# Odd third row-maximum tile of an attention loop, taken as two half-width tiles in opposite row halves

## The chip, the cores and the metric

The kernel runs on one core of a Trainium2 chip. The metric is device time in microseconds (us) of one execution. Its engines run side by side and meet at semaphores: TensorE (PE, whose weight loads the profile lists apart as PEld), VectorE (DVE), ScalarE (ACT), GpSimd (POOL) and SyncE (SP), which issues most DMAs. Matmuls write to PSUM, which the kernel divides into eight tiles of 128 partitions by 512 fp32 numbers. They are called banks below.

## The reference

```python
x = A_x                                            # 1 x 2048 x 640
g = sigmoid((x * gate_w).sum(-1, keepdims=True))
q, k, v = heads(x @ wqkv)                          # 32 heads of 20 columns
a = softmax(q @ k.T * 20 ** -0.5) @ v @ wo         # per head, 2048 queries x 2048 keys
u = gelu(einsum("bsd,sf->bdf", layernorm(x), w1) + b1)   # over the token axis, 1728 wide
b = einsum("bdf,fs->bds", u, w2) + b2
return g * a + (1 - g) * transpose(b)
```

Everything is fp32. The kernel writes a number as the sum of a high and a low part of a shorter type (fp32r) where the product must stay exact.

## The kernel before

The kernel has four stages: the projections q, k and v; the token MLP; the attention loop; and the output projection. The 32 heads are treated as 16 pairs (`NP`). The two heads of a pair (`j` = 0 and 1) lie in rows 0 to 63 and 64 to 127 of every stacked operand, so a matmul of head 0 uses the upper half of TensorE's rows and one of head 1 the lower half. Such matmuls can run beside each other.

**Scores twice.** The softmax subtracts each query's maximum. The scores are therefore computed once with queries on the partitions, only to find the maximum ("s" tiles, line 178: 128 queries by 512 keys, reduced along the keys by VectorE on line 180). They are computed a second time with keys on the partitions ("st" tiles, line 700), with the negative maximum as two extra rows of the operand, and go to ScalarE for the exponential (line 703). The results `p` are multiplied with v (line 637, "pv"). A pair has 128 s tiles in two halves of queries (64 each), four key chunks (`kc`) for each of eight query tiles (`t`), and two heads. The maxima go to `mx`, are folded by `s_max` (lines 139 to 146), transposed by `s_store`, stored to DRAM and loaded by `load_m` as rows of the operand of the st matmuls.

**The stream of s tiles.** `s_tiles` (line 167) is a generator of closures. Each issues one matmul and one reduction, and `s_next` (line 155) runs the next one, then counts down the delayed steps in `s_close`. The first 736 of the 2048 tiles (`S_AHEAD`) are issued in the MLP, two at a time between the MLP's matmuls. The remaining 1312 (`LEFT`) are issued in the attention loop.

**The attention loop.** It has 16 pairs by 32 iterations, each with four st tiles (two heads `j` by two query chunks `c`) and four exponentials. `take` s tiles are put between the st tiles: 344 iterations take three, 140 take two, and the last 28 none. `turn` (line 708) keeps the row halves of successive matmuls alternating when an odd number was issued. After the four st tiles `pv_flush` issues eight pv matmuls with the exponentials of the iteration before. These use all 128 rows. Every 16th iteration a pv accumulation ends and `pv_evac` (line 618) copies it out on VectorE.

**Order and banks.** TensorE, VectorE, ScalarE, GpSimd and SyncE run in the order in which the code is written, so a waiting instruction holds all that is behind it on its engine. Of the eight banks `st_tile` has four, `s_tile` three, and pv one. A pool hands its banks round in turn: the fourth s tile counted from a given one takes its bank again, and its matmul waits for the reduction of the former tile. In an iteration with `take` under three, the third st tile takes a bank of the s pool, so that this pool is used three times in each iteration that takes two or three.

The lines that matter are these:

```python
def s_tile(shape, name):
    return psum.tile(shape, F32, tag="s", bufs=3, name=name)
...
for n in range(4):
    st_op((n + turn) % 2, n // 2, s_tile if n == 2 and take < 3 else st_tile)
    if n < take:
        s_next()
```

Of the kernel before, what the change touches and what calls it, by code (L numbers as in the profile page):

```python
# [7 lines left out]
F32 = mybir.dt.float32  # L8
F32R = mybir.dt.float32r
AF = mybir.ActivationFunctionType  # L10
OP = mybir.AluOpType
AX = mybir.AxisListType

P = 128
S, D, H, DH, F = 2048, 640, 32, 20, 1728
# [13 lines left out]
def gated_mix(ctx, tc, xT, x, wqk, wv0, wv1, wo, w1, w1t, b1, w2, b2, out):  # L29
    nc = tc.nc  # L30
# [5 lines left out]
    def hi_lo(hi, lo, src, hi_eng=None, lo_eng=None):  # L36
        if hi_eng is nc.scalar:
            nc.scalar.activation(hi, src, AF.Copy)  # L38
        else:
            (hi_eng or nc.vector).tensor_copy(hi, src)  # L40
        (lo_eng or nc.vector).tensor_sub(lo, src, hi.bitcast(F32))  # L41
# [22 lines left out]
    cp = ctx.enter_context(tc.tile_pool(name="cp", bufs=1))  # L64
# [3 lines left out]
    def st_tile(shape, name):  # L68
        return psum.tile(shape, F32, tag="st", bufs=4, name=name)

    def s_tile(shape, name):
        return psum.tile(shape, F32, tag="s", bufs=3, name=name)
# [44 lines left out]
    def base_stack(p, full, eng=nc.sync):  # L117
        ks = k8([P, S], F32R, f"ks{p}_{full}")
        qs = [q4([P, S // 2], F32R, f"qs{p}_{full}_{i}") for i in range(2)]
        load_stack(p, ks, qs, full, eng)  # L120
        return ks, qs

    def load_m(p, qs, half, put=nc.sync.dma_start):
        src = m_d[p, half].rearrange("(g i j t) r -> i j t g r", i=2, j=2, t=8)
        for j in range(2):
            for i in range(2):
                r = 64 * j + 3 * DH + i
                dst = qs[half].bitcast(F32)[r: r + 1, :].rearrange("o (t g r) -> o t g r", g=4, r=32)
                put(dst, src[i: i + 1, j])

    s_src, st_src, v_tiles = {}, {}, {}

    def load_v(p):
        v_tiles[p] = base.tile([P, NT, NPAIR], F32, tag="v", bufs=2, name=f"v{p}")
        c0 = NPAIR * (p % 8)
        nc.sync.dma_start(v_tiles[p], v_d[p // 8, :, :, c0: c0 + NPAIR].rearrange("t p c -> p t c"))

    s_close = []

    def s_max(p, half, mx):  # L140
        mm = cp.tile([P, 16], F32, tag="mm", bufs=2, name=f"mm{p}_{half}")
        mc = cp.tile([P, 32], F32R, tag="mc", bufs=2, name=f"mc{p}_{half}")
        nc.vector.tensor_reduce(mm, mx.rearrange("p k j t -> p (j t) k"), axis=AX.X, op=OP.max)
        nc.gpsimd.tensor_scalar_mul(mm, mm, -1.0)
        hi_lo(mc[:, :16], mc[:, 16:], mm, hi_eng=nc.gpsimd, lo_eng=nc.gpsimd)
        s_close.append([8, lambda: s_store(p, half, mc)])

    def s_store(p, half, mc):
        mt = cp.tile([P, 32], F32, tag="mt", bufs=2, name=f"mt{p}_{half}")
        nc.vector.transpose(mt, mc.bitcast(F32))  # L150
        s_close.append([M_LAG[0], lambda: m_queue[0].dma_start(m_d[p, half], mt)])

    M_LAG = [8]

    def s_next():
        next(stream)()
        for e in list(s_close):
            e[0] -= 1
            if e[0] <= 0:
                s_close.remove(e)  # L160
                e[1]()

    def s_finish():
        next(stream, None)
        while s_close:
            s_close.pop(0)[1]()

    def s_tiles(p):
        for half in range(2):
            mx = cp.tile([P, 4, 2, 8], F32, tag="mx", bufs=2, name=f"mx{p}_{half}")  # L170
            for t in range(8):
                for kc in range(4):
                    for j in (1, 0):
                        def f(j=j, kc=kc, t=t):
                            ks, qs = s_src[p]
                            ps = s_tile([P, 512], f"s{p}_{half}_{t}_{j}_{kc}")
                            r = slice(64 * j, 64 * j + 3 * DH)
                            nc.tensor.matmul(ps, qs[half][r, t * P:(t + 1) * P], ks[r, kc * 512:(kc + 1) * 512],  # L178
                                             start=True, stop=True)
                            nc.vector.tensor_reduce(mx[:, kc, j, t: t + 1], ps, axis=AX.X, op=OP.max)  # L180
                        yield f
            s_close.append([2, lambda p=p, half=half, mx=mx: s_max(p, half, mx)])

    def s_stream(on_start):
        for p in range(NP):
            on_start(p)
            yield from s_tiles(p)

    hooks = [None]
    m_queue = [nc.gpsimd]  # L190
    stream = s_stream(lambda p: hooks[0](p))

    p1s = ExitStack()
# [99 lines left out]
    for half in range(2):  # L293
        wvh, wvl = wvs[half]
        width = HALF + 2 if half == 0 else HALF
        for t in range(NT):
            n = NT * half + t
# [9 lines left out]
            ps = st_tile([P, width], f"v{half}_{t}")  # L307
# [256 lines left out]
    while done < S_AHEAD:  # L564
        s_next()
        done += 1
# [7 lines left out]
    def s_stack(p):  # L574
        ks = lp.tile([P, S], F32R, tag="sk", bufs=2, name=f"sk{p}")
        qs = [lp.tile([P, S // 2], F32R, tag="sq", bufs=4, name=f"sq{p}_{i}") for i in range(2)]
        load_stack(p, ks, qs, False)
        return ks, qs
# [52 lines left out]
    def pv_flush():  # L631
        while pend:
            p, qh, kt, pv, pts = pend.pop(0)
            for j in range(2):
                for c in range(2):
                    r = 32 * (2 * j + c)
                    nc.tensor.matmul(pv[r: r + 32, :], v_tiles[p][:, kt, 10 * j: 10 * j + 32], pts[j, c],  # L637
                                     start=(kt == 0), stop=(kt == NT - 1))
            if kt == NT - 1:
                pv_evac(p, qh, pv)  # L640
# [4 lines left out]
    def load_wo(c):  # L645
        raw = ap.tile([P, D], F32, tag="wor", bufs=1, name=f"wor{c}")
        nc.gpsimd.dma_start(raw, wo[c * P:(c + 1) * P, :])
        hi_lo(woh[c], wol[c], raw, hi_eng=nc.gpsimd, lo_eng=nc.gpsimd)
# [15 lines left out]
    def o_early(q, hi_eng=nc.scalar, lo_eng=nc.vector):  # L664
        o_hl[q] = o_part(q, slice(0, (NC - 1) * P), NC - 1, 256, "e", 2, hi_eng, lo_eng)
# [1 line left out]
    def o_late(q):  # L667
        return o_part(q, slice((NC - 1) * P, D), 1, 512, "l", 4, nc.scalar, nc.vector)[0]

    turn = given = 0  # L670
    LEFT = NP * 128 - S_AHEAD
    for p in range(NP):
        ks, qs = st_src[p]
        if 8 <= p < 8 + NC:
            load_wo(p - 8)
        for it in range(32):
            qh, kt = divmod(it, NT)
            if p + 1 < NP:
                if it == 6:
                    st_src[p + 1] = base_stack(p + 1, True)  # L680
                if it == 12:
                    load_v(p + 1)
                if it == 27:
                    load_m(p + 1, st_src[p + 1][1], 0)
            if it == 11 and p:
                load_m(p, qs, 1)
            if it == 14 and due_stack:
                n = due_stack.pop()
                if n < NP:
                    s_src[n] = s_stack(n)  # L690
            if p == NP - 1 and it in (20, 26):
                o_early(it // 26, nc.gpsimd, nc.gpsimd)
            if kt == 0:
                pv = psum.tile([P, 512], F32, tag="pv", bufs=1, name=f"pv{p}_{qh}")
            pts = {}

            def st_op(j, c, tile):
                r = slice(64 * j, 64 * j + 3 * DH + 2)
                ps = tile([P, 512], f"st{p}_{it}_{j}{c}")
                nc.tensor.matmul(ps, ks[r, kt * P:(kt + 1) * P], qs[qh][r, c * 512:(c + 1) * 512],  # L700
                                 start=True, stop=True)
                pt = lp.tile([P, 512], F32, tag="pt", bufs=12, name=f"p{p}_{it}_{j}{c}")
                nc.scalar.activation(pt, ps, AF.Exp, scale=SCALE)  # L703
                pts[j, c] = pt

            due = min((p * 32 + it + 1) * LEFT // (NP * 32 - 28) + 1, LEFT)
            take = min(due - given, 3)
            for n in range(4):
                st_op((n + turn) % 2, n // 2, s_tile if n == 2 and take < 3 else st_tile)
                if n < take:  # L710
                    s_next()
            given += take
            if take and given == LEFT:
                s_finish()
            turn = (turn + take) % 2
            pv_flush()
            if p * 32 + it in later:
                later.pop(p * 32 + it)()
            pend.append((p, qh, kt, pv, pts))
# [19 lines left out]
    for t in range(NT):  # L739
# [5 lines left out]
        ps = [st_tile([P, HALF], f"a{t}_{i}") for i in range(2)]  # L745
        a_mms(t, ps, o_hl[t // 2], slice((t % 2) * P, (t % 2 + 1) * P), range(NC - 1))
    for t in range(NT):
        ps = [st_tile([P, HALF], f"b{t}_{i}") for i in range(2)]
# [49 lines left out]
```

## Time and profile before

| | us |
|---|---|
| median of 3 runs (1844.1 to 1847.46) | 1844.79 |
| span of the profiled execution | 1844.8 |
| s tiles start (in the MLP) | 227 |
| attention loop, first to last exponential | 700 to 1762 |
| last reduction of an s tile | 1706 |
| PE busy, PEld busy | 1829.7, 1135.2 |
| VectorE busy, ScalarE busy, GpSimd busy | 1428.9, 1361.6, 637.1 |

The profiled execution is as long as the median run. TensorE shows as busy nearly throughout, but the end of a matmul is modelled and two matmuls in opposite row halves overlap, so this share says little of how full it is. The starts of the weight loads, one ahead of each matmul, show better how the matmuls follow each other. In the views, a line gives an engine, the line of the code, the operation, the tile written and those read, its shape, and how often it ran; times are in us, means of one instruction in ns. "Idle before" is the time that the engine stood still ahead of the instruction, with what ended it.

### The profile page before, as it was taken

Reading aid. Unit: us, or ns where it says so; the run is one execution under the profiler, and the core shown is the slowest. Engines: PE = TensorE matmul, PEld = TensorE weight load, DVE = VectorE, ACT = ScalarE, POOL = GpSimd, SP = SyncE. Lnnn points to the kernel's source line nnn. Section 1 sums busy time; section 2 is a strip of 40 time slices with the busy share of each in tenths; the row PEclk is TensorE's granted clock in tenths of the full one; section 3 lists DMA queues with packets and bytes.
Section 4 is the critical chain, followed back from the end, with each engine's and each line's share of the span. In section 5 each row is a group of like instructions: output and inputs, shape, how many; then the busy total and the mean of one; then the engine's idle time right before and its main releaser. Section 6 shows DMA issues by size and latency. Waiting matters only on the chain. (4 is left out here: it accounts for less than half of the span.)

```text
span 1844.8 us, 39129 instructions
## 1 busy us (share of the span) xinstructions
PE 1829.7 (99%) x14978; PEld 1135.2 (62%) x14978; DVE 1428.9 (77%) x2341; ACT 1361.6 (74%) x2688; POOL 637.1 (35%) x900
## 2 busy tenths in 40 slices
PE   9999999999999999999999999999999999999998
PEld 7998799999999994333333333333333333333378
DVE  4202299999999998888888888888888888888137
ACT  4243244465444448999999999999999999999930
POOL 1013478888887770112112111121321211212210
PEclk9999999999999999999999999999999999999999
DMA  8456766566645645504032324213540423301463
GB/s 289 143 169 212 222 173 173 158 194 193 168 139 166 189 136 121 118 15 103 20 85 61 73 42 93 57 50 78 107 103 24 109 47 77 71 14 23 131 219 132
DMA packets 152831, 216.61 MB, mean 117 GB/s; under 512 B 65698, under 2 KB 92082, under 8 KB 148738
## 3 DMA queue, kind: packets, MB, share of 16 engines
q1 hardware_dynamic: 129172, 178.68, 35.4%
q0 software_dynamic: 14688, 20.78, 5.2%
q10 hardware_dynamic: 8784, 14.65, 2.4%
q8 instruction: 118, 1.93, 0.4%
q14 instruction: 69, 0.57, 0.1%
HBM read 165.43 MB, written 48.25 MB: 116 GB/s over the span
## 5 line engine op out<-in xcount | busy, mean ns | idle before, releaser
L180 DVE TENSOR_REDUCE mx<-s 128x1 f32<-128x512 f32 x2048 | 1293.7, 684 | 159.9 <-PE s L178 119.7
L703 ACT ACTIVATE p<-st 128x512 f32<-128x512 f32 x2048 | 1042.1, 615 | 20.9 <-PE s L178 2.2
L700 PEld LDWEIGHTS st<-qs_True,ks_True 62*128 62x128 f32 x2048 | 307.3, 185 | 485.1 <-ACT p L703 312.9
L700 PE MATMUL st<-qs_True,ks_True 62*128 62x512 f32 x2048 | 579.6, 425 | 0.2 <-ACT ty L477 0.2
L637 PE MATMUL pv<-p,v 128*32 128x512 f32 x4096 | 555.5, 605 | 0.2
L178 PE MATMUL s<-sk,sq 60*128 60x512 f32 x1280 | 423.1, 434 | 0.0
L41 POOL TENSOR_TENSOR wl<-wr,wh 128x512 fp32r<-128x512 f32 x228 | 273.6, 1216 | 59.8 <-ACT wh L38 30.9
L624 POOL DMA_DIRECT2D o_d<-oev x128 | 67.0, 524 | 494.3 <-DVE oev L618 491.6
L178 PE MATMUL s<-ks_False,qs_False 60*128 60x512 f32 x768 | 225.1, 397 | 0.4 <-DVE mx L180 0.3
L46 PE MATMUL y<-gh,wh 64*128 64x320 f32 x896 | 216.8, 308 | 0.0
L46 PE MATMUL y<-gl,wh 64*128 64x320 f32 x832 | 210.3, 306 | 0.0
L46 PE MATMUL y<-gh,wl 64*128 64x320 f32 x832 | 209.4, 305 | 0.0
L38 ACT ACTIVATE wh<-wr 128x512 fp32r<-128x512 f32 (+2 forms) x246 | 135.9, 594 | 90.2 <-PE s L178 29.0
L178 PEld LDWEIGHTS s<-sk,sq 60*128 60x128 f32 x1280 | 197.7, 185 | 1.2
L637 PEld LDWEIGHTS pv<-p,v 128*32 128x32 f32 x4096 | 84.9, 108 | 171.4 <-issue 156.4
L46 PE MATMUL u<-hl,wh 64*128 64x320 f32 x864 | 167.1, 306 | 0.0
L46 PE MATMUL u<-hh,wh 64*128 64x320 f32 x864 | 167.1, 306 | 0.0
L46 PE MATMUL u<-hh,wl 64*128 64x320 f32 x800 | 156.9, 306 | 0.4 <-POOL wl L41 0.4
L46 PEld LDWEIGHTS y<-gh,wh 64*128 64x128 f32 x896 | 155.3, 184 | 0.4
L46 PEld LDWEIGHTS y<-gh,wl 64*128 64x128 f32 x832 | 147.0, 184 | 0.3
L46 PEld LDWEIGHTS y<-gl,wh 64*128 64x128 f32 x832 | 146.9, 184 | 0.0
L178 PEld LDWEIGHTS s<-ks_False,qs_False 60*128 60x128 f32 x768 | 124.4, 184 | 1.1 <-DVE mx L180 1.1
(124 smaller groups left out, 1817.6 us busy)
## 6 DMA issues: line engine op xcount, KB each, us to landing
wr<-in_w_dram SPq DMA_DIRECT2D x196, 256.0 KB
ks_True<-k_d SPq DMA_DIRECT2D x96, 160.0 KB
qs_True<-q_d SPq DMA_DIRECT2D x192, 80.0 KB
sk<-k_d SPq DMA_DIRECT2D x60, 160.0 KB
sq<-q_d SPq DMA_DIRECT2D x120, 80.0 KB
v_d<-vt SPq DMA_DIRECT2D x32, 168.0 KB
v<-v_d SPq DMA_DIRECT2D x16, 336.0 KB
xr<-in_xT_dram SPq DMA_DIRECT2D x20, 256.0 KB
```

Source lines behind the costliest of these rows:

```text
L38: nc.scalar.activation(hi, src, AF.Copy)
L41: (lo_eng or nc.vector).tensor_sub(lo, src, hi.bitcast(F32))
L46: nc.tensor.matmul(ps[k], a[r], b[r], start=start, stop=stop)
L178: nc.tensor.matmul(ps, qs[half][r, t * P:(t + 1) * P], ks[r, kc * 512:(kc + 1) * 512], start=True, stop=True)
L180: nc.vector.tensor_reduce(mx[:, kc, j, t: t + 1], ps, axis=AX.X, op=OP.max)
L624: nc.gpsimd.dma_start(o_d[DH * h: DH * h + DH, cols], ev[r: r + DH, :])
L637: nc.tensor.matmul(pv[r: r + 32, :], v_tiles[p][:, kt, 10 * j: 10 * j + 32], pts[j, c], start=(kt == 0), stop=(kt == NT - 1))
L700: nc.tensor.matmul(ps, ks[r, kt * P:(kt + 1) * P], qs[qh][r, c * 512:(c + 1) * 512], start=True, stop=True)
L703: nc.scalar.activation(pt, ps, AF.Exp, scale=SCALE)
```

## The change

An iteration that takes three s tiles now takes one full pair (both heads of one key chunk) and one half pair: 256 keys of head 0 ahead of the first st tile and the same 256 keys of head 1 behind the last one. The order in such an iteration is half (head 0), st 1, st 0, s 1, s 0, st 1, st 0, half (head 1), pv. An iteration that takes two has st 1, st 0, s 1, s 0, st 1, st 0, pv. The four st tiles always use the four banks of `st_tile`; `turn` is gone. Every tile of the s pool, a half one too, takes one of its three banks.

Only the chunks `kc` 2 and 3 are ever halved. `mx` has six columns of maxima instead of four, and a full tile of these chunks is reduced to two maxima in one instruction. Units with `kc` under 2 that `s_half` meets first are set aside in `s_skipped` and issued as the next full ones. The MLP uses the same `s_next`, so it issues the same tiles in the same order, with two-result reductions for half of them.

```diff
-    def s_next():
-        next(stream)()
+    def s_tick():
         for e in list(s_close):
             e[0] -= 1
             ...
+    def s_next():
+        if not s_one:
+            s_one.extend(s_full(s_skipped.pop(0) if s_skipped else next(stream)))
+        s_one.pop(0)()
+        s_tick()
...
+    def s_full(u):
+        def f(j):
+            ps = s_tile([P, 512], f"s{u.p}_{u.half}_{u.t}_{j}_{u.kc}")
+            u.mm(ps, j, 0, 512)
+            if u.kc < 2:
+                nc.vector.tensor_reduce(u.mx[:, u.kc, j, u.t: u.t + 1], ps, axis=AX.X, op=OP.max)
+            else:
+                nc.vector.tensor_reduce(u.mx[:, 2 * u.kc - 2: 2 * u.kc, j, u.t],
+                                        ps.rearrange("p (a b) -> p a b", a=2), axis=AX.X, op=OP.max)
+            u.ended(2)
+        return [lambda j=j: f(j) for j in (1, 0)]
+
+    def s_half():
+        while not s_rest:
+            u = next(stream)
+            if u.kc < 2:
+                s_skipped.append(u)
+            else:
+                s_rest.extend([(u, 0), (u, 1)])
+        u, h = s_rest.pop(0)
+
+        def f(j):
+            ps = s_tile([P, 256], f"s{u.p}_{u.half}_{u.t}_{j}_{u.kc}_{h}")
+            u.mm(ps, j, 256 * h, 256)
+            nc.vector.tensor_reduce(u.mx[:, 2 * u.kc - 2 + h, j, u.t: u.t + 1], ps, axis=AX.X, op=OP.max)
+            u.ended(1)
+
+        f(0)
+
+        def close():
+            f(1)
+            s_tick()
+
+        return close
...
+                mx = cp.tile([P, 6, 2, 8], F32, tag="mx", bufs=2, name=f"mx{p}_{half}")
...
-            for n in range(4):
-                st_op((n + turn) % 2, n // 2, s_tile if n == 2 and take < 3 else st_tile)
-                if n < take:
+            close = s_half() if take % 2 else None
+            for c in range(2):
+                for j in (1, 0):
+                    st_op(c, j)
+                if c == 0 and take > 1:
+                    s_next()
                     s_next()
+            if close:
+                close()
             given += take
             if take and given == LEFT:
                 s_finish()
-            turn = (turn + take) % 2
             pv_flush()
```

More of the change, by code (lines that the diff above doesn't have):

```diff
@@ L161, in s_next @@
                 e[1]()
+    def s_next():
[3 more added lines that the diff above has]
+        s_tick()
     def s_finish():
-        next(stream, None)
+        assert not s_one and not s_rest and not s_skipped
         while s_close:
             s_close.pop(0)[1]()
[L168 to L182, printed above, removed]
@@ new lines, in gated_mix, with __init__, mm, ended @@
+    s_one, s_rest, s_skipped = [], [], []
+    class Unit:
+        def __init__(self, p, half, t, kc, mx, left):
+            self.p, self.half, self.t, self.kc, self.mx, self.left = p, half, t, kc, mx, left
+        def mm(self, ps, j, lo, n):
+            ks, qs = s_src[self.p]
+            r = slice(64 * j, 64 * j + 3 * DH)
+            k0 = self.kc * 512 + lo
+            nc.tensor.matmul(ps, qs[self.half][r, self.t * P:(self.t + 1) * P], ks[r, k0: k0 + n], start=True,
+                             stop=True)
+        def ended(self, n):
+            self.left[0] -= n
+            if self.left[0] == 0:
+                s_close.append([2, lambda: s_max(self.p, self.half, self.mx)])
@@ L186, in s_stream @@
             on_start(p)
-            yield from s_tiles(p)
+            for half in range(2):
+                mx = cp.tile([P, 6, 2, 8], F32, tag="mx", bufs=2, name=f"mx{p}_{half}")
+                left = [128]
+                for t in range(8):
+                    for kc in range(4):
+                        yield Unit(p, half, t, kc, mx, left)
     hooks = [None]
@@ L668, in o_late @@
         return o_part(q, slice((NC - 1) * P, D), 1, 512, "l", 4, nc.scalar, nc.vector)[0]
-    turn = given = 0
+    given = 0
     LEFT = NP * 128 - S_AHEAD
@@ L695, in gated_mix, with st_op @@
             pts = {}
-            def st_op(j, c, tile):
+            def st_op(c, j):
                 r = slice(64 * j, 64 * j + 3 * DH + 2)
-                ps = tile([P, 512], f"st{p}_{it}_{j}{c}")
+                ps = st_tile([P, 512], f"st{p}_{it}_{j}{c}")
                 nc.tensor.matmul(ps, ks[r, kt * P:(kt + 1) * P], qs[qh][r, c * 512:(c + 1) * 512],
```

## Prediction

> **What bounds the kernel now.** I read the page's first part, then a table of stretches, then the groups and waits of 900 to 1700 us, and last the weight loads of single iterations.
>
> ```profile
> PE 1829.7 (99%) x14978; PEld 1135.2 (62%) x14978; DVE 1428.9 (77%) x2341; ACT 1361.6 (74%) x2688; POOL 637.1 (35%) x900
> ```
>
> ```profile
> core 0: us, PE busy (x) PEld busy (x) DVE busy (x) ACT busy (x) POOL busy (x), PEclk, DMA share, GB/s
> 900.00:1700.00 800.00, 799.94 (x5663) 309.70 (x5663) 678.40 (x1107) 784.56 (x1540) 150.84 (x302) 1.00 0.30 65
> 1706.50:1745.00 38.50, 38.38 (x244) 11.59 (x240) 3.82 (x6) 38.50 (x80) 12.11 (x16) 1.00 0.36 115
> ```
>
> The page's shares average over four stages; the change acts in the attention loop, so its stretch is read alone. TensorE is busy without a gap there at a granted clock of 1.00, and ScalarE for 98%. An iteration has four exponentials: 1540 are 385 iterations, 2.078 us each. Without s tiles (last stretch, about 20 iterations) four exponentials take some 1.93 us, so ScalarE is no bound until an iteration falls to about 1.93.
>
> ```profile
> L703 ACT ACTIVATE p<-st 128x512 f32<-128x512 f32 x1540 | 785.4, 604 | 15.4 <-PE s L178 0.9
> L180 DVE TENSOR_REDUCE mx<-s 128x1 f32<-128x512 f32 x1044 | 660.4, 683 | 120.6 <-PE s L178 91.9 <-PE st L700 26.4
> L618 DVE COPY oev<-pv 128x512 f32<-128x512 f32 x24 | 16.4, 682 | 1.0 <-PE pv L637 1.0
> ```
>
> ```profile
> PEld st L700 <- ACT p L703: 248.5, 370, 0.8
> PEld pv L637 <- issue: 116.5, 367, 0.4
> ...
> PEld st L700 <- DVE mx L180: 4.3, 17, 0.4
> ```
>
> VectorE waits for TensorE (120.6 us); TensorE's loads wait for VectorE only 17 times. The 248.5 us put down to ScalarE need a second look: they are the pause of 0.84 us behind the pv matmuls, and that pause is equally long where it is put down to "issue". It is the pv work itself. The loads of single iterations show this (start, length, engine, line):
>
> ```profile
> 1203.84 0.18 PEld L700 LDWEIGHTS st<-qs_True,ks_True 62*128 62x128 f32 x1 [0.84 <-ACT p L703]
> ...
> 1204.47 0.19 PEld L700 LDWEIGHTS st<-qs_True,ks_True 62*128 62x128 f32 x2 [0.34 <-DVE mx L180]
> 1204.91 0.16 PEld L637 LDWEIGHTS pv<-p,v 128*32 128x32 f32 x8 [0.25 <-issue]
> 1205.90 0.18 PEld L700 LDWEIGHTS st<-qs_True,ks_True 62*128 62x128 f32 x1 [0.84 <-issue]
> 1205.90 0.29 PEld L178 LDWEIGHTS s<-sk,sq 60*128 60x128 f32 x2
> 1206.01 0.41 PEld L700 LDWEIGHTS st<-qs_True,ks_True 62*128 62x128 f32 x2
> 1206.25 0.19 PEld L178 LDWEIGHTS s<-sk,sq 60*128 60x128 f32 x1
> 1206.48 0.18 PEld L700 LDWEIGHTS st<-qs_True,ks_True 62*128 62x128 f32 x1
> 1207.02 0.16 PEld L637 LDWEIGHTS pv<-p,v 128*32 128x32 f32 x8 [0.35 <-issue]
> 1208.02 0.18 PEld L700 LDWEIGHTS st<-qs_True,ks_True 62*128 62x128 f32 x1 [0.84 <-ACT p L703]
> ...
> 1210.15 0.18 PEld L700 LDWEIGHTS st<-qs_True,ks_True 62*128 62x128 f32 x1 [0.84 <-ACT p L703]
> ...
> 1211.05 0.16 PEld L637 LDWEIGHTS pv<-p,v 128*32 128x32 f32 x8 [0.34 <-issue]
> 1212.05 0.18 PEld L700 LDWEIGHTS st<-qs_True,ks_True 62*128 62x128 f32 x1 [0.84 <-issue]
> ...
> 1213.22 0.16 PEld L637 LDWEIGHTS pv<-p,v 128*32 128x32 f32 x8 [0.24 <-issue]
> 1214.22 0.18 PEld L700 LDWEIGHTS st<-qs_True,ks_True 62*128 62x128 f32 x1 [0.84 <-ACT p L703]
> ```
>
> An iteration is a score part, up to the pv load, and a pv part of 1.00 us (1207.02 to 1208.02, 1211.05 to 1212.05). The iteration from 1205.90 takes three s tiles: its seven matmuls go through the row halves as 0.23 us steps (loads at 1206.01, 1206.25, 1206.48), the seventh alone in its half. Its score part is 1.12 us, the whole 2.12; the next one, behind a two-tile iteration, takes 2.17 (1212.05 to 1214.22). I call these odd. The even one from 1210.15 has three pairs: 0.90 and 1.90. The mean of the odd follows from the stretch: 1044 reductions in 385 iterations are 2.71 each, so 71% are odd, and (2.078 − 0.29 × 1.90) / 0.71 = 2.15 us. **The bound is TensorE's score part**, with the lone seventh matmul in it.
>
> **The change part by part.**
>
> *Half a step less on TensorE.* With two half tiles each row half holds 3.5 matmuls, not 4 and 3. What 256 columns cost is read from matmuls of 320 and 512 in the MLP (300 to 690 us):
>
> ```profile
> L46 PE MATMUL y<-gh,wh 64*128 64x320 f32 x865 | 209.1, 307 | 0.0
> L178 PE MATMUL s<-ks_False,qs_False 60*128 60x512 f32 x610 | 183.0, 393 | 0.0
> ```
>
> 86 ns for 192 columns are 115 ns for 256. If nothing waited, an odd iteration would fall from 2.12 to 2.01 us.
>
> *A new wait.* The s pool has three banks and an odd iteration now uses four tiles of it: half 0, s 1, s 0, half 1. So half 1 always takes the bank that half 0 of the same iteration filled, and its matmul waits until VectorE has reduced that; in the built program its wait is for just that reduction. Before, three tiles used three banks, and each bank's former tile was an iteration old. I follow the wait from the first load, with these rows of VectorE:
>
> ```profile
> 1206.47 0.69 DVE L180 TENSOR_REDUCE mx<-s 128x1 f32<-128x512 f32 x1 [0.78 <-PE s L178]
> ```
>
> ```profile
> 1203.14 1.27 DVE L180 TENSOR_REDUCE mx<-s 128x1 f32<-128x512 f32 x2
> ```
>
> ```profile
> L315 DVE COPY gs<-v 128x2 f32<-128x2 f32 x16 | 2.5, 159 | 28.9 <-ACT vt L312 28.9
> ```
>
> 1. Start of the reduction of half 0: the s tile loaded at 1205.90 reached an idle VectorE at 1206.47, 0.57 later. With 256 columns less that is 0.455.
> 2. Its length is not in the trace. Copies out of PSUM take 682 ns for 512 elements and 159 for 2, thus 1.03 ns an element; 0.69 less 256 of these is 0.43, ended at 0.885. The outer ends are 0.25 (the fold of 64 numbers, quoted below, less than half its data) and 0.69 (no saving).
> 3. Release: the reduction that ended at 1203.14 + 1.27 = 1204.41 let the load of 1204.47 go, 0.06 later by these rounded rows. So half 1 loads at about 0.94. Unhindered it would load near 0.57, where the matmul ahead of it in its half begins.
> 4. From a held load to the pv load behind it: 1204.47 to 1204.91, 0.44, less 0.115: 0.325. The score part is then 1.26, and with the pv part 1.00 the iteration is **2.25 us** (2.24 to 2.26 by the rounding) against 2.15.
>
> Behind half 1 in TensorE's order stand the eight pv matmuls and all of the next iteration, so the wait is paid in full. VectorE doesn't carry a backlog that lengthens it: reductions follow each other at 0.60 (1.27 less 0.68, nearly), thus half ones at about 0.34, and s 1 and s 0 (ready from 0.8) and half 1 are done near 2.36, 0.11 into the next iteration, ahead of 0.455. So 344 × (2.25 − 2.15) = +34 us.
>
> The Trainium skill ("VectorE: DVE Perf Modes", the section on the TRN2 errata) gives VectorE 120 cycles plus one per element from PSUM at 0.96 GHz and advises tiles of 512 or more, as each small one pays the fixed part; that speaks against halves. By its figure a half takes 392 ns (an estimate), and the sum would be some 12 us lower. For 512 it gives 658 ns where the rows have 683, so I keep 0.43.
>
> *VectorE's copy ahead of half 0.* Every 16th iteration copies the pv result at the start of the next:
>
> ```profile
> 1201.95 0.68 DVE L618 COPY oev<-pv 128x512 f32<-128x512 f32 x1
> 1202.55 1.27 DVE L180 TENSOR_REDUCE mx<-s 128x1 f32<-128x512 f32 x2
> ```
>
> That iteration began at 1201.71, so reducing began at 0.84. Before, no matmul waited for it. Now half 0 starts there in place of 0.455, and half 1 is held 0.38 longer. 21 of the 31 such iterations are odd by the code's own rule of `take`: +8 us.
>
> *Even iterations.* The third st tile no longer takes a bank of the s pool. The waits of 4.3 us in 800 go; half of a 0.34 idle time is the normal cadence. I take −3 us over the loop. In exchange the four st banks wait for ScalarE: the first starts about 0.56 into an even iteration, the fourth ends 3 × 0.48 + 0.60 later, 0.70 into the next odd one, and the st tile that needs the bank would load at 0.46. That can delay its matmul to 0.85, but half 1 behind it is held to 0.94 in any case; if that cover were gone, 140 × 0.04 (the 2.17 beside 2.12) = 6 us would show.
>
> *Nothing from the rest.* The 172 halved units come from `kc` 2 and 3; each odd iteration still advances the stream by three tiles, and `s_tick` runs as often, so folds, transposes, m_d stores on GpSimd's queue and `load_m` on SP's move by an iteration or two; a single wait of 0.8 us for a load of m_d stands in the 800 us. The 344 added reductions fill VectorE's idle 120.6 us partly; that they cost no more is reckoned above. In the MLP, reductions with two results are new:
>
> ```profile
> L180 DVE TENSOR_REDUCE mx<-s 128x1 f32<-128x512 f32 x611 | 385.0, 685 | 4.3 <-PE s L178 0.5
> L143 DVE TENSOR_REDUCE mm<-mx 128x16 f32<-128x64 f32 x10 | 2.6, 256 | 0.0
> ```
>
> VectorE is 99% busy there (385 of 390 us, one in 0.638 against 0.61 back to back). 16 results of 64 numbers take 256 ns, so one result more costs a few ns: nothing. At the other end a second result costs another 159 ns, half the reductions slow the mean to 0.69, and 736 × 0.05 = 37 us come on top.
>
> **Sum** against the profiled execution (1844.8, equal to the median of the runs): 1844.8 + 34 + 8 − 3 = **1884 us**.
>
> **Rivals.**
>
> *Slower, as forecast, by 20 to 60 us: 0.82.* For it: the bank rule and five measured steps.
>
> *The wait is covered: faster.* If half 1's load were let go by 0.57 to 0.70, odd iterations would be 2.01 us, above ScalarE's 1.93, and the time 1844.8 − 344 × 0.14 − 3 = 1794 us. The deciding point is a load at 0.83: there the iteration is 0.83 + 0.325 + 1.00 = 2.15, as long as before. Against it: VectorE can start on half 0 only at 0.455, which leaves 0.37 for a reduction with its release, and my estimate is 0.49. With the outer end 0.25 the load is at 0.765, the iteration 2.09, and the total about 1829. Chance of such times 0.08.
>
> *The wait nearly evens out:* 1841 to 1849, 0.03.
>
> *Two results are dear in the MLP:* +37, thus 1921 us; against it the fold's row. 0.04. Still longer waits (VectorE carrying a backlog, a half reduction near 0.69, up to 344 × 0.26 = 90 us more): 0.03.
>
> *The change does something else:* it can't be void, since 344 more reductions and other bank uses are in the program; its cost stands in the rivals above.
>
> **How the numbers follow.** The likeliest case gives 1884. A half reduction between 0.39 and 0.46 moves it from 1870 to 1894; 0.02 us of error in each of the other three steps adds 7 us either way, and the copies may cost 0 to 12. The range 1864 to 1904 holds the main case but for its edges, about 0.8 of the chance. A measurement can tell about 0.2% (3.7 us). Faster by more than that 0.08, within 0.03, slower 0.89.
>
> **What would show it.** In the changed profile the weight loads of s (half 1) wait for the reduction, about 344 times and 0.3 us each, where 17 waits stood before; the score part of an odd iteration is about 1.26, its pv part still 1.00, an even one 1.89. Reductions of 256 take near 0.43; TensorE's loop is some 40 us longer; VectorE idles at the start of each odd iteration. The MLP ends at the same time. A half 1 that loads without a gap, or a pv part that shrinks, would prove me wrong.

## The result and the profile after

The changed kernel takes 1871.59 us (median of 4 runs, 1870.35 to 1872.37); the kernel before took 1844.44 in the same comparison. The ratio is 1.0142, 95% interval 1.0124 to 1.0159: slower by 27 us. The forecast was 1884 us, a loss of 39.

The page's first part and the stretch from 900 to 1700 us of the changed kernel (columns as in the prediction's table of stretches):

```profile
PE 1854.3 (99%) x15322; PEld 1202.2 (64%) x15322; DVE 1459.1 (78%) x2685; ACT 1361.5 (73%) x2688; POOL 636.8 (34%) x900
```

```profile
900.00:1700.00 800.00, 798.04 (x5783) 350.58 (x5782) 684.59 (x1347) 763.28 (x1501) 150.75 (x302) 1.00 0.30 65
```

There are 344 matmuls and reductions more, as the code says. TensorE is still shown as busy throughout, which does not say how full it is. ScalarE tells the loss: 1501 exponentials in 800 us where there were 1540, so an iteration takes 2.132 us on average, not 2.078. The waits of TensorE's weight loads in that stretch say for what:

```profile
PEld s L183 <- DVE mx L196: 137.8, 166, 0.8
PEld st L747 <- ACT p L750: 114.2, 210, 0.8
PEld s L183 <- DVE mx L198: 71.4, 86, 0.8
PEld s L183 <- DVE mx L215: 40.0, 161, 0.6
```

Line 215 is the new reduction of a half tile. The rows of up to 0.8 us are the pause behind pv once more, now put down to other engines. The row of line 215 counts 161 holds and 40 us. That is less than all: in the odd iterations right behind an even one (139 of 342 in the loop) the st load just ahead comes late too, waiting 0.21 us on average for ScalarE, so the held load follows it without idle time and is not counted. The time from the end of the opening half's reduction to the closing half's load shows that all are held: its median over the odd iterations is 54 ns, and nine tenths of them lie at 53 or 54. One odd iteration and the even one behind it, in weight loads and then in VectorE's instructions:

```profile
1223.22 0.18 PEld L183 LDWEIGHTS s<-sk,sq 60*128 60x128 f32 x1 [0.84 <-DVE mx L198]
1223.22 0.29 PEld L747 LDWEIGHTS st<-qs_True,ks_True 62*128 62x128 f32 x2
1223.33 0.31 PEld L183 LDWEIGHTS s<-sk,sq 60*128 60x128 f32 x2
1223.56 0.35 PEld L747 LDWEIGHTS st<-qs_True,ks_True 62*128 62x128 f32 x2
1224.12 0.18 PEld L183 LDWEIGHTS s<-sk,sq 60*128 60x128 f32 x1 [0.21 <-DVE mx L215]
1224.43 0.16 PEld L684 LDWEIGHTS pv<-p,v 128*32 128x32 f32 x8
1225.42 0.19 PEld L747 LDWEIGHTS st<-qs_True,ks_True 62*128 62x128 f32 x2 [0.84 <-ACT p L750]
...
1226.32 0.16 PEld L684 LDWEIGHTS pv<-p,v 128*32 128x32 f32 x8 [0.26 <-issue]
1227.31 0.18 PEld L183 LDWEIGHTS s<-sk,sq 60*128 60x128 f32 x1 [0.84 <-DVE mx L196]
```

```profile
1223.64 0.42 DVE L215 TENSOR_REDUCE mx<-s 128x1 f32<-128x256 f32 x1 [0.24 <-PE s L183]
1223.99 1.29 DVE L196 TENSOR_REDUCE mx<-s 128x1 f32<-128x512 f32 x2
1225.19 0.41 DVE L215 TENSOR_REDUCE mx<-s 128x1 f32<-128x256 f32 x1
```

The opening half loads at 1223.22. VectorE, idle for 0.24, starts its reduction at 1223.64 and ends it at 1224.06. The closing half loads at 1224.12, and pv at 1224.43. The score part is 1.21 where it was 1.12 and 1.17 in the two odd iterations shown of before; the pv part is 0.99 and the whole 2.20.

Sorting all iterations by what they take (from the first pv load of one to the first pv load of the next; the score part in between decides the class) gives the whole account. Each cell is a mean in us; the differences are count times difference:

| iterations | count | before | after | difference |
|---|---|---|---|---|
| odd | 321 | 2.152 | 2.208 | +18 |
| odd, behind a copy of pv | 21 | 2.148 | 2.534 | +8 |
| even | 140 | 1.913 | 1.899 | −2 |
| last 28, no s tile | 28 | 1.941 | 2.041 | +3 |

The sum of the loop is +27 us. The loop's first pv load lies at 700 to 704 us in all the profiles of this study (702 before, 700 after), so the MLP with its two-result reductions is as long as it was; this scatter of some 2 us is most of why the spans (1844.8 and 1868.6) differ by 24 only. The profiled execution of the changed kernel took 1870.35 us, 1.8 more than its span. If the same holds for the kernel before, its profiled execution took about 1846.6 us, some 2 us more than the median run, and was not as long as it. The prediction's base hardly suffers: 1844.8 is 0.4 above the median of this comparison.

### The profile page after: what moved, and what is told of

It is laid out like the page before. It is cut to its first block, busy times and chain, and to the rows that moved or that the text cites. A ratio compares the mean times of both kernels' runs of the same rounds, so it can differ in the third digit from the quotient of the medians.

```text
span 1868.6 us, 39987 instructions
## 1 busy us (share of the span) xinstructions
PE 1854.3 (99%) x15322; PEld 1202.2 (64%) x15322; DVE 1459.1 (78%) x2685; ACT 1361.5 (73%) x2688; POOL 636.8 (34%) x900
## 5 line engine op out<-in xcount | busy, mean ns | idle before, releaser
L196 DVE TENSOR_REDUCE mx<-s 128x1 f32<-128x512 f32 x1024 | 659.4, 685 | 50.6 <-PE s L183 48.9
L747 PE MATMUL st<-qs_True,ks_True 62*128 62x512 f32 x2048 | 554.3, 436 | 0.1
L183 PE MATMUL s<-sk,sq 60*128 60x512 f32 (+1 forms) x1614 | 467.7, 389 | 1.9 <-DVE mx L215 0.4
L198 DVE TENSOR_REDUCE mx<-s 128x2 f32<-128x512 f32 x680 | 436.4, 687 | 29.8 <-PE s L183 27.4
L183 PEld LDWEIGHTS s<-sk,sq 60*128 60x128 f32 x1614 | 229.2, 185 | 332.8 <-DVE mx L196 172.2
L215 DVE TENSOR_REDUCE mx<-s 128x1 f32<-128x256 f32 x688 | 288.1, 419 | 74.6 <-PE s L183 73.3
L183 PE MATMUL s<-ks_False,qs_False 60*128 60x512 f32 (+1 forms) x778 | 240.7, 393 | 0.4 <-DVE mx L196 0.3
L46 PE MATMUL u<-hl,wh 64*128 64x320 f32 x864 | 188.1, 306 | 0.0
L46 PE MATMUL u<-hh,wh 64*128 64x320 f32 x864 | 188.0, 306 | 0.0
L46 PE MATMUL u<-hh,wl 64*128 64x320 f32 x800 | 177.6, 306 | 0.1
```

The source lines that it names most:

```text
L46: nc.tensor.matmul(ps[k], a[r], b[r], start=start, stop=stop)
L183: nc.tensor.matmul(ps, qs[self.half][r, self.t * P:(self.t + 1) * P], ks[r, k0: k0 + n], start=True, stop=True)
L196: nc.vector.tensor_reduce(u.mx[:, u.kc, j, u.t: u.t + 1], ps, axis=AX.X, op=OP.max)
L198: nc.vector.tensor_reduce(u.mx[:, 2 * u.kc - 2: 2 * u.kc, j, u.t], ps.rearrange("p (a b) -> p a b", a=2), axis=AX.X, op=OP.max)
L215: nc.vector.tensor_reduce(u.mx[:, 2 * u.kc - 2 + h, j, u.t: u.t + 1], ps, axis=AX.X, op=OP.max)
```

## The experiments

The theory: the closing half waits for the reduction of the opening half, whose bank it takes. The main rival: the cost comes from the added work (VectorE's 344 more reductions, or half-width matmuls that aren't half as long), not from the place of one wait. Runs of the kernel before beside these experiments have medians of 1845 to 1846 us. Five of the kernels have one run each; for them the profile's iterations carry the argument more than the total.

**Without the opening half's reduction.**

```diff
-            nc.vector.tensor_reduce(u.mx[:, 2 * u.kc - 2 + h, j, u.t: u.t + 1], ps, axis=AX.X, op=OP.max)
+            c = u.mx[:, 2 * u.kc - 2 + h, j, u.t: u.t + 1]
+            if j:
+                nc.vector.tensor_reduce(c, ps, axis=AX.X, op=OP.max)
+            else:
+                nc.vector.memset(c, -1e30)
```

> The changed kernel without the reduction of the opening half tile (head 0): its matmul stays, its 256 scores per query go into no maximum, and VectorE sets that column to -1e30 instead. So the closing half tile no longer waits for VectorE. Theory (the closing half is held by the opening half's reduction): odd iterations fall from 2.21 to about 2.01 us, those behind a copy of pv from 2.53 to about 2.01 too, 321 x 0.20 + 21 x 0.52 = 75 us less than the changed kernel, about 1797 us. Rival (the cost is something else in the odd iteration, such as a half-width matmul that takes as long as a full one, or ScalarE): odd iterations stay above 2.13 and the time above 1840 us.

Measured: 1834.38 us (1830.82 to 1835.9), 0.9932 of before, interval 0.9914 to 0.9949. The hold is gone and with it 37 us, not the 75 expected. An odd iteration, in weight loads:

```profile
1225.55 0.18 PEld L183 LDWEIGHTS s<-sk,sq 60*128 60x128 f32 x1 [0.84 <-DVE mx L198]
1225.55 0.29 PEld L751 LDWEIGHTS st<-qs_True,ks_True 62*128 62x128 f32 x2
1225.66 0.30 PEld L183 LDWEIGHTS s<-sk,sq 60*128 60x128 f32 x2
1225.89 0.50 PEld L751 LDWEIGHTS st<-qs_True,ks_True 62*128 62x128 f32 x2
1226.21 0.18 PEld L183 LDWEIGHTS s<-sk,sq 60*128 60x128 f32 x1
1226.63 0.16 PEld L688 LDWEIGHTS pv<-p,v 128*32 128x32 f32 x8 [0.23 <-issue]
```

The second pair of st loads spans 0.50 us (0.35 in the changed kernel): its last load comes at 1226.21 in place of about 1226.06, and the closing half follows at once. So another wait took the place of the one removed. The shortest odd score parts are 1.01, the value worked out for an unhindered one; the mean odd iteration is 2.06, the even one has risen to 2.02. Both are near the 2.04 of the last 28 iterations of the changed kernel, which have no s tiles at all. That pointed to the other part of the change: the st tiles, which go to the exponentials, have four banks in every iteration.

**More work for VectorE, at two places.**

```diff
+            if j == 0:          # in the other kernel: j == 1
+                nc.vector.tensor_reduce(extra, ps[:, :64], axis=AX.X, op=OP.max)
             nc.vector.tensor_reduce(u.mx[:, 2 * u.kc - 2 + h, j, u.t: u.t + 1], ps, axis=AX.X, op=OP.max)
```

> The changed kernel with one more VectorE reduction of 64 of the opening half tile's columns, ahead of the real one (344 more instructions; the result isn't used). Theory: VectorE is idle when this half arrives, so the release of the closing half moves by what one such instruction takes, estimated 0.15 to 0.22 us from the copy of 2 elements (159 ns) and 1.03 ns an element; odd iterations 2.36 to 2.43, 50 to 75 us more than the changed kernel. Rival (VectorE's total load counts, not its place): the same time as with the extra reduction on the closing half.

> The changed kernel with the same extra reduction of 64 columns, but on the closing half tile: equal work for VectorE, at a place behind which no matmul waits, since VectorE has about 0.3 us to spare before the next opening half arrives. Theory: no change, 1868 to 1876 us. Rival (VectorE's total load counts): 50 us or more above the changed kernel.

Measured in one run each: 1918.97 us with the extra reduction on the opening half, 1878.28 on the closing one. The loads of an odd iteration with it on the opening half:

```profile
1220.15 0.18 PEld L184 LDWEIGHTS s<-sk,sq 60*128 60x128 f32 x1 [0.84 <-DVE mx L197]
...
1221.18 0.18 PEld L184 LDWEIGHTS s<-sk,sq 60*128 60x128 f32 x1 [0.38 <-DVE mx L218]
1221.49 0.16 PEld L687 LDWEIGHTS pv<-p,v 128*32 128x32 f32 x8
```

```profile
1220.57 0.23 DVE L217 TENSOR_REDUCE extra<-s 128x1 f32<-128x64 f32 x1 [0.25 <-PE s L184]
1220.71 0.42 DVE L218 TENSOR_REDUCE mx<-s 128x1 f32<-128x256 f32 x1
```

The reduction that the closing half waits for starts 0.14 later (1220.57 to 1220.71, as the two overlap), and so do the closing half's load (1.03 into the iteration, was 0.90) and the pv load. Odd iterations average 2.339, up by 0.131. On the closing half the same work leaves them at 2.211; the loop is 3 us longer, 2 of it in the iterations behind a copy, and the rest of the 7 us is scatter outside the loop (it starts 3 us later). The total load isn't the cause, its place is. My estimate of the extra time was a little high (0.15 to 0.22), so the first kernel came out 3 us below its range; the second came out 2 us above its own.

**The copy of pv, and the last 28 iterations.**

```diff
             take = min(due - given, 3)
+            if it % 16 == 1:
+                take = min(take, 2)
...
-                    st_op(c, j)
+                    st_op(c, j, s_tile if take == 0 and c and j else st_tile)
```

> The changed kernel with two edits that act in different iterations, so that its profile tells them apart: the iteration at whose start VectorE copies a finished pv takes two tiles instead of three (the third follows later), and in the last 28 iterations, which take none, the fourth st tile uses a bank of the s pool. Theory: 21 iterations of 2.53 us turn into usual ones of 2.21 (7 us less); the 28 fall from 2.04 back towards 1.94 (3 us less); together about 1862 us. Rival (the copy delays TensorE by pv's bank, not by the opening half; the last iterations are slow for want of ScalarE, not of banks): no change.

Measured: 1868.84 us (1867.46 to 1869.25), 1.0123 of before (1.0108 to 1.0138). The last 28 iterations return to 1.939 us. The 21 iterations of 2.53 are gone: the odd ones that stand in for them take 2.208, but the even ones with the copy take more than 1.90: 1.94 behind an odd iteration (22 of them) and 2.18 behind another even one (8). So 4 us came of it and not 7. The loop is 7 us shorter where 10 were expected, and the time only 3: the loop of this profile starts 2.5 us later, and 1868.84 misses the expected 1862 in part by such scatter. In the stretch without s tiles ScalarE's count shows the second part (changed kernel first, then this one; the columns as above):

```profile
1730.00:1768.50 38.50, 38.50 (x229) 12.74 (x228) 3.17 (x4) 38.10 (x77) 11.66 (x14) 1.00 0.36 115
```

```profile
1725.00:1763.50 38.50, 38.36 (x244) 11.86 (x241) 5.95 (x11) 38.22 (x79) 11.87 (x19) 1.00 0.34 102
```

77 exponentials, then 79 in the same 38.5 us: with a fifth bank ScalarE gets through more, though its work is the same.

**The opening half behind the first st tile.** This asks for the 0.035 us by which the reduction started sooner than worked out.

```diff
                 for j in (1, 0):
                     st_op(c, j)
+                    if first and c == 0 and j:
+                        first()          # the opening half
```

> The changed kernel with the opening half tile behind the first st tile instead of ahead of it; nothing else is moved. Question: why the reduction of the opening half began 0.42 us after its load where 0.455 was worked out from a tile that ended together with an st tile. Theory A (a matmul reports its end in program order, so a half tile behind a full one ends only with it): the reduction starts about 0.57 after the load, odd iterations 2.21 + 0.15 = 2.36, about 1922 us. Theory B (each row half reports by itself): within 0.03 of before the swap, 1870 to 1882 us.

Measured in one run: 1921.96 us, theory A's figure; that it fits to the microsecond is luck, as the loop is 48 us longer than the changed kernel's and starts 2.6 us later. Odd iterations take 2.358 (2.36 expected). VectorE starts 0.56 after the half's load, as for a full tile:

```profile
1222.01 0.18 PEld L745 LDWEIGHTS st<-qs_True,ks_True 62*128 62x128 f32 x1 [0.84 <-ACT p L748]
1222.02 0.29 PEld L183 LDWEIGHTS s<-sk,sq 60*128 60x128 f32 x2
```

```profile
1222.58 0.43 DVE L215 TENSOR_REDUCE mx<-s 128x1 f32<-128x256 f32 x1 [0.40 <-PE st L745]
```

The wait is now put down to the st tile. A half tile that follows a full one in the program is passed on only with it, though it runs in the other row half.

**Four banks alone, in the kernel before.**

```diff
-                st_op((n + turn) % 2, n // 2, s_tile if n == 2 and take < 3 else st_tile)
+                st_op((n + turn) % 2, n // 2, st_tile)
```

> The kernel before with one part of the change alone: all st tiles use the four banks of their own pool; the third s tile stays whole. Theory: even iterations 1.90 instead of 1.91 (no wait for VectorE, 2 us less), the last 28 go from 1.94 to 2.04 (3 us more), odd ones keep 2.15: 1844 to 1849 us, no difference that can be measured. Rival (four banks slow ScalarE in every iteration): 1860 us or more.

Measured: 1848.23 us (1845.85 to 1850.62), 1.0017 of before (1.0007 to 1.0027). The last 28 take 2.040 as expected, the even ones 1.941, more than before (1.913) and not less, the odd ones 2.137, a little less: +4, −5 and +3 us, so 1.5 us in all. Nearly the whole −5 lies in the odd iterations right behind an even one (2.169 before, 2.136 here); an even one and the odd one behind it take 4.08 together in both kernels.

**No third tile, with four banks and with five.**

```diff
-            ps = s_tile([P, 256], f"s{u.p}_{u.half}_{u.t}_{j}_{u.kc}_{h}")
-            u.mm(ps, j, 256 * h, 256)
-            nc.vector.tensor_reduce(u.mx[:, 2 * u.kc - 2 + h, j, u.t: u.t + 1], ps, axis=AX.X, op=OP.max)
+            nc.vector.memset(u.mx[:, 2 * u.kc - 2 + h, j, u.t: u.t + 1], -1e30)
...
-                    st_op(c, j)          # the second kernel alone
+                    st_op(c, j, s_tile if c and j else st_tile)
```

> The changed kernel without the halved tiles in the attention loop: 688 matmuls and reductions of 256 keys are left out (VectorE sets their maxima to -1e30), so each of the first 484 iterations has two s tiles and four st tiles. TensorE alone would allow 1.89 us an iteration. Theory (with four banks for the exponentials ScalarE's round through a bank sets a floor, which is why the run without the hold stayed at 2.02 to 2.06): 2.02 to 2.05 an iteration, about 1825 us. Rival (that run was limited by something else of the odd iterations): 1.89 to 1.95, about 1775 us.

> As the run without the halved tiles, with the third st tile of every iteration in a bank of the s pool (the same work left out). Theory (the floor is one of banks): 1.91 to 1.96 an iteration, ScalarE back to back, about 1780 us. Rival (the floor is ScalarE's own time or TensorE's): the same time as with four banks.

Measured in one run each: 1828.71 us with four banks, 1790.66 with five. The two stretches from 900 to 1700 us:

```profile
900.00:1700.00 800.00, 800.00 (x5488) 323.13 (x5486) 525.40 (x1384) 792.74 (x1572) 155.00 (x311) 1.00 0.30 68
```

```profile
900.00:1700.00 800.00, 799.86 (x5663) 299.94 (x5660) 526.06 (x1378) 799.74 (x1633) 162.79 (x318) 1.00 0.32 72
```

ScalarE shows as busy 99% in the first and still runs 4% fewer exponentials: 1572 are 2.036 us an iteration, 1633 are 1.960. So four banks set a floor of about 2.04 though TensorE alone would allow 1.89, and five one of 1.96, which is ScalarE back to back (799.74 busy of 800 us). It is a floor of the mean: even iterations of the changed kernel take 1.90, between odd ones of 2.21. The rival (1775 us with four banks) is out; my 1780 for five was 11 too low, as the floor is 1.96 and not 1.93.

No version beats the kernel before with its work complete. One bank shared by both halves, with one reduction behind the second, was not tried, so no run shows whether it would work or help.

## Why the prediction was right

**The bound.** TensorE's score part sets the pace of the odd iterations, as read from the loads. That is shown by the closing half: what holds it lengthens each iteration by nearly the same amount (0.13 of 0.14 us).

**The new wait** is the cause, and its five terms can be compared one by one. Start of the reduction 0.42 (0.455), its length 0.42 (0.43), release to the load 0.05 to 0.06 (0.06), load to pv 0.31 (0.325), pv part 0.99 to 1.00 (1.00): 2.20 to 2.21 for 2.25. The prediction's terms as written add up to 2.27 and not to the 2.25 that it went on with; with 2.27 the forecast would have been 1891, so this slip brought it 7 us closer by luck. **The start was mis-sized**: the row that I scaled was a tile that ended with an st tile ahead of it in the program. The swap shows that a half tile behind a longer one is passed on later, and the half that leads the iteration does not pay that. That a full tile behind an equally long one pays the 0.035 for the same reason is argued and not shown. The step from the held load to pv was read from two st loads let go together (0.44); the lone held st load of the odd iterations right behind an even one took 0.425 in the kernel before (median), and less 0.115 that is the 0.31 measured. The length and the release were high by no more than the rounding of the rows. As the odd iterations of before took 2.152, the loss is 0.056 each and not 0.10, thus 19 us over 342, not 34. An error of 2% in the new iteration's length was nearly half of the difference that counts.

**VectorE's copy** cost 0.326 each (2.534 less 2.208), 7 us, for the 8 predicted. One such iteration opens at 1210.28; its reduction starts 0.75 behind that (0.84 predicted), behind the copy:

```profile
1210.42 0.69 DVE L665 COPY oev<-pv 128x512 f32<-128x512 f32 x1
1211.03 0.41 DVE L215 TENSOR_REDUCE mx<-s 128x1 f32<-128x256 f32 x1
```

```profile
1211.49 0.18 PEld L183 LDWEIGHTS s<-sk,sq 60*128 60x128 f32 x1 [0.56 <-DVE mx L215]
```

**Even iterations** gained 2 us of the 3.

**The last 28 iterations** were missed. They lost 3 us because the change takes their fifth bank away, and giving it back brought 2.04 down to 1.94; the code says so (`take` under three), and I counted only the iterations with s tiles.

**The rest cost nothing**, as forecast: 680 two-result reductions take 687 ns where the one-result ones take 685, and the MLP is not longer. By the PSUM figure of the Trainium skill ("VectorE: DVE Perf Modes", the section on the TRN2 errata) the half reduction would take 392 ns, an estimate. Here 688 of them take 419, near the row-derived 0.43:

```profile
L215 DVE TENSOR_REDUCE mx<-s 128x1 f32<-128x256 f32 x688 | 288.1, 419 | 74.6 <-PE s L183 73.3
L198 DVE TENSOR_REDUCE mx<-s 128x2 f32<-128x512 f32 x680 | 436.4, 687 | 29.8 <-PE s L183 27.4
```

**The faster rival** was priced wrongly. With the wait gone the time is 1834 and not 1794, because ScalarE's bound was taken from iterations that had five banks. Its floor with four, 2.04, would have been the next wait. The prediction did see that the four st banks wait for ScalarE, and rightly that the hold covers this; but it put what would show without that cover at 6 us, where 2.06 and 2.02 against the 2.01 and 1.90 worked out are some 34.

What stays open: the means of the unheld kernel (2.06 and 2.02) are explained by the floor of four banks, but the round through the banks wasn't followed instruction by instruction; and which wait moves from the odd iteration to the even one ahead of it when the kernel before loses its fifth bank was not followed.

## What to carry to other kernels

Count the tiles of a stage against the banks of its pool before counting columns: a fourth tile on three banks waits for the first of the same round, however short it is, and everything behind it in order waits too. An engine's floor holds for the buffers that it had where it was read; when a change takes one away, read the floor anew. Scale a latency only from a row whose neighbours are like the new instruction's, and if the answer is the difference of two near numbers, expect its error to be large.

## What the runs showed of the hardware

A short matmul in one row half, issued behind a longer one in the other, handed its result on only with the longer (reduction 0.56 us after its load, 0.42 when it was issued ahead). The Trainium skill ("TensorE: Matmul & The Clock Gate", Part 3 on packing small matmuls) says that matmuls end in program order. The swap agrees, at a cost of 48 us in the loop. Reducing 512 numbers from PSUM to two results cost 2 ns more than to one. A reduction of 64 took 0.22 us, of 256 0.42, of 512 0.685, but issued back to back the one of 64 delayed the next by 0.14 only.
